# Two of three bit patterns of a key tile summed by an accumulating GpSimd transfer

## The chip, the cores and the metric

The kernel runs on one core of one Trainium2 chip. The metric is the device time of one execution in microseconds. Engines go by their names or by the profile's short ones: TensorE (PE, its weight loads PEld), VectorE (DVE), ScalarE (ACT), GpSimd (POOL) and SyncE (SP, which here only issues transfers).

## The reference

The input x is 2048 rows of 512. It is layer-normalised (no scale, no shift), and the result xn feeds two branches whose product is added to x:

```
q = xn @ wq     32 heads of 16       k, v = xn @ wk, xn @ wv     one head of 16, shared by all 32
s = softmax(q k^T / 4) v, heads joined, @ wo
g = silu( silu(xn @ w1) @ w2 )       w1: 512 x 1792, w2: 1792 x 512
out = x + s * g
```

All inputs and the output are bf16. The large part is the softmax: 32 heads x 2048 queries x 2048 keys, each score exponentiated once.

## The kernel before, in words

The attention is cut into 32 groups: four chunks of 512 queries, and in each eight groups of four heads. A group has 16 key tiles of 128 keys. A **key tile** of a group is four blocks, one a head, each 128 keys x 512 queries. Scores lie transposed (keys on partitions), so a block of exponentials multiplies V directly: a product is one matmul with a 128 x 32 weight (16 columns of V, the rest ones that sum the denominator), and the four heads' products run side by side in four column strips of TensorE. Four such products together are called a quad here. They add up in one PSUM bank per group (`psO`).

A key tile's exponentials are made in one of two ways.

- **ScalarE's tiles.** TensorE writes the scores of two heads into a pair of PSUM banks (`psA`, two pairs in turn, line 613), ScalarE turns 1024 columns at a time into bf16 (`exp_A`, line 643, into one of 11 pieces of `pa_sb`). A tile is two such instructions, and four products, one quad.
- **VectorE's tiles.** TensorE writes one head's scores into one of three banks (`D`, `D1` of `psD`, and `F` = `psF`, which dense work uses too). VectorE adds a constant, clips at zero and writes int16 (`exp_D`, line 681). Read as bf16 these bits are a piecewise linear 2^x. GpSimd adds a constant to the bits of the four blocks at once (`shift`, line 706), once for each of two further patterns, which are the same curve with its kinks elsewhere. The three patterns are weighted and added: each has its own copy of V, scaled by `PH_W`, in `vaug_sb`. So such a tile takes twelve products, three quads. The three patterns of a tile lie in one of `NPD = 4` pattern tiles: three in `ph_sb`, and a fourth in parts of `x_sb` once these are free (`free_slot`, `ph_ap`).

The order of all instructions is written out in Python before the program is built. `Sched.op` appends an instruction to its engine's queue and derives the semaphore waits from what it reads and writes; `Sched.model` keeps an estimated clock for each engine, with fixed costs. A loop at the end goes from one ScalarE exponential to the next: `score_run` sends a burst with ScalarE's next scores and, for heads that are left, scores of VectorE's tiles into free banks (`fill_D`, which starts a new tile through `next_D`); `emit_PV` sends products that the estimated clock says are ready; the rest of TensorE's time goes to the dense jobs (both layers of the gate branch, q projections, the output projection), all in bank `F`. `advance_v` chooses VectorE's next instruction. Parameters of these choices are switched every 5 us of estimated time by a string of letters (`PLAN`, `RULES`). The engines run their queues in order, so what stands in the order is kept on the chip.

Names that matter for the change: `owe` records that a product is still to be made (weight copy `v`, where its block lies, from when it is ready), `owed` and `planned` count the products of a group, `plan_D` adds those of a VectorE tile when it is started. `front` is the list of layer-norm, transposition and k/v work of the start. `left[g]` lists the key tiles of group g that nobody has taken; ScalarE takes from its beginning and VectorE from its end, VectorE only while more than three are left (one in the last group), else from the next group.

Of the kernel before, what the change touches and what calls it, by code (L numbers as in the profile page):

```python
# [6 lines left out]
ALU = mybir.AluOpType  # L7
AX = mybir.AxisListType
FP32 = mybir.dt.float32
BF16 = mybir.dt.bfloat16  # L10
# [5 lines left out]
NQ = 512  # L16
# [3 lines left out]

PH_SHIFT = (0, 43, 85)
PH_W = (0.2265625, 0.1787109375, 0.1416015625)
PH_ONE = 127 * 128
PH_BIAS = 65
NPH = len(PH_SHIFT)
LN2 = 0.6931471805599453
QSCALE = 0.25 * 128.0 / LN2
ESCALE = LN2 / 128.0  # L30
# [5 lines left out]
class Sched:  # L36
# [5 lines left out]
    def __init__(self):  # L42
        self.queues = {}
        self.done = {}
        self.clock = {}
        self.snap = {}
        self.last_w = {}
        self.readers = {}
        self.flagged = {}
        self.lanes = {}  # L50
        self.at = {}
        self.free = dict(pe=1.2, a=1.7, v=0.85, gp=0.7, sp=0.7)
        self.act_end = 0.0
        self.act_ends = []
        self.pe_mode, self.pe_last, self.pe_len, self.pe_tiles = None, 1.0, 0.0, set()
        self.pe_runs = []
        self.gp_runs, self.tt_runs = [], []

    def deps(self, eng, reads, writes):
        deps = {}  # L60
# [33 lines left out]
        return self.pe_last + self.pe_len + (self.SWITCH if mode != self.pe_mode else 0.003)  # L94

    def model(self, eng, lane, cost, r):
        if lane:
            t = max(self.free[eng], r) + 0.05
            self.free[eng] = t
            return t + (cost or 3.0)  # L100
        if eng == "pe":
            mode, tiles, cols = cost or ("full", [None] * 4, 128)
            t = r
            for tile in tiles:
                if mode != self.pe_mode:
                    t = max(t, self.pe_last + self.pe_len + self.SWITCH)
                    self.pe_tiles = set()
                elif tile is not None and tile not in self.pe_tiles:
                    t = max(t, self.pe_last + 0.004)
                else:  # L110
                    t = max(t, self.pe_last + self.pe_len + 0.003)
                    self.pe_tiles = set()
                self.pe_tiles.add(tile)
                self.pe_mode, self.pe_last, self.pe_len = mode, t, max(cols, 60) / 2400.0
                self.pe_runs.append((t, t + self.pe_len))
            self.free[eng] = t
            return t + cols / 2400.0 + self.FLY + self.SEM
        if eng == "a":
            n = cost or 512
            t = max(r, self.free["a"], self.act_end - 0.428)  # L120
            self.free["a"] = t
            self.act_end = max(t + 0.3 + n / 1200.0, self.act_end + 0.0635 + n / 1200.0)
            return self.act_end + self.SEM
        t = max(r, self.free[eng] - (0.084 if eng == "v" else 0.0))
        if eng == "v" and isinstance(cost, tuple):

            t = max(r, self.free[eng] - 0.13)
            end = t + cost[0]
            for a, b in self.gp_runs[-6:]:
                if a < t - 0.1:  # L130
                    end = max(end, b + cost[0] - 0.13)
            self.tt_runs.append((t, end))
            self.free[eng] = end
            return end + self.SEM
        end = t + (cost or 0.4)
        if eng == "gp" and cost and cost > 1.0:
            for a, b in self.tt_runs[-3:]:
                if a <= t + 0.1 and b > t:
                    end = max(end, b + 0.89)
            self.gp_runs.append((t, end))  # L140
        self.free[eng] = end
        return end + self.SEM
# [71 lines left out]
def bass_recurrent_scan__grouped_kv_mqa__dense_activation_silu__prompt_kernel(  # L214
# [22 lines left out]
    assert (S, D, F) == (2048, 512, 1792)  # L237

    NPA = 11
    NPD = 4  # L240
    NPS = 3
    NGN = 2
# [50 lines left out]
    with ExitStack() as es:  # L293
# [46 lines left out]
        K = Sched()  # L340
# [290 lines left out]
        def owe(gi, i, kt, v, ap, key, at, half=None):  # L631
            pend[gi].append(dict(i=i, kt=kt, v=v, ap=ap, key=key, at=at, half=half))
# [40 lines left out]
        def ph_key(j, sl, p):  # L673
            return ("ph", j, sl, p) if sl < 3 else ("x", 4 * j + p)

        def exp_D(blks):

            tile, idx, pos, bank = blks[0]["tile"], blks[0]["idx"], blks[0]["pos"], blks[0]["bank"]
            sl, m = slot_of[idx], 512 * len(blks)
            src = bank_ap(bank, m)  # L680
            d = op("v", lambda e: e.tensor_scalar(ph_ap(0, sl, 512 * pos, 512 * pos + m), src,  # L681
                                                  float(PH_ONE + PH_BIAS), 0.0, op0=ALU.add, op1=ALU.max),
                   reads=[b["bank"] for b in blks], writes=[ph_key(0, sl, b["pos"]) for b in blks],
                   cost=1.221 if len(blks) == 2 else 0.687)
            for b in blks:
                p = b["pos"]
                owe(tile[0], b["i"], tile[1], 1, ph_ap(0, sl, 512 * p, 512 * p + 512).bitcast(BF16), ph_key(0, sl, p), K.at[d])
                hold[b["bank"]] = None
                rows_of.setdefault(idx, {})[p] = b["i"]
            if len(rows_of[idx]) == len(blks[0]["rows"]):  # L690
                if ("ag", NC - 1) in tok:
                    shift(tile, idx)
                else:
                    shifts.append((tile, idx))

        shifts = []

        def shift(tile, idx):
            sl, n = slot_of[idx], len(rows_of[idx])
            for j in range(1, NPH):  # L700
                if n < 4:
                    d = op("v", lambda e, j=j: e.tensor_scalar(ph_ap(j, sl, 0, NQ * n), ph_ap(0, sl, 0, NQ * n), float(PH_SHIFT[j]), None,
                                                               op0=ALU.add),
                           reads=[ph_key(0, sl, p) for p in range(n)], writes=[ph_key(j, sl, p) for p in range(n)], cost=0.4)
                else:
                    d = op("gp", lambda e, j=j: e.int64_add(ph_ap(j, sl, 0, 4 * NQ).bitcast(I64), ph_ap(0, sl, 0, 4 * NQ).bitcast(I64),  # L706
                                                            PH_SHIFT[j] * 0x0001000100010001),
                           reads=[ph_key(0, sl, p) for p in range(4)], writes=[ph_key(j, sl, p) for p in range(4)], cost=1.03)
                for p, i in rows_of[idx].items():
                    owe(tile[0], i, tile[1], 1 + j, ph_ap(j, sl, 512 * p, 512 * p + 512).bitcast(BF16), ph_key(j, sl, p), K.at[d])  # L710

# [67 lines left out]
                state["g"] += 1  # L779
            return n  # L780

        def plan_D(gi, rows):
            owed[gi] += len(rows) * (NPH - 1)
            for i in rows:
                planned[gi][i] += NPH - 1

# [519 lines left out]
        def fill_D(t, free, only=None):  # L1308
# [9 lines left out]
            for bank in banks[:max(0, len(banks) - keep)]:  # L1318
                pick = [(o, i) for o in dst["open"] for i in o["todo"] if i in free]
                if not pick:  # L1320
                    pick = [(o, o["todo"][0]) for o in dst["open"] if o["tile"][0] < group_A() or len(left[o["tile"][0]]) < F_LATE]
                if not pick and len(dst["open"]) < 2:
                    new, rows = next_D(t), [0, 1, 2, 3]
                    if new is not None:
                        left[new[0]].remove(new[1])
                    else:
                        new, rows = next_half(t), [0, 1]
                    if new is not None:
                        plan_D(new[0], rows)
                        dst["idx"] += 1  # L1330
                        slot_of[dst["idx"]] = free_slot(new[0])
                        dst["open"].append(dict(tile=new, todo=list(rows), rows=rows, idx=dst["idx"]))
                        pick = [(dst["open"][-1], i) for i in free if i in rows] or [(dst["open"][-1], rows[0])]
                if not pick:
                    return
                o, i = pick[0]
                pos = len(o["rows"]) - len(o["todo"])
                o["todo"].remove(i)
                if not o["todo"]:
                    dst["open"].remove(o)  # L1340
                burst([((o["tile"], i), bank_ap(bank))], [bank])
                dst["fifo"].append(dict(tile=o["tile"], i=i, bank=bank, idx=o["idx"], pos=pos, rows=o["rows"]))
                hold[bank] = "blk"
                if i not in free:
                    return
                free.remove(i)
                if not free:
                    return
# [171 lines left out]
```

## Time and profile before

| | |
|---|---|
| median of 3 runs | 662.22 us (661.94 to 662.23) |
| the profiled execution | 662.46 us, of it span 660.6 us |
| TensorE clock granted | 1.000 |
| ScalarE exponentials (L643) | 662 of 1024 columns, 630.5 us busy |
| VectorE pattern instructions (L681) | 714, for 724 blocks = 181 key tiles |
| GpSimd shifts (L706) | 362, 374.8 us busy |
| TensorE products (L765) | 2172 of patterns, 1332 of ScalarE's blocks |
| DMA | 12.48 MB, all issued by SP and ACT |

An engine's busy time is the union of its instructions. Matmuls overlap: one takes 383 ns from start to end, but the four of a quad run together and the next quad starts 0.22 us after, so TensorE's 98% counts more than what it could not have done otherwise. In a group's row the figures after the bar are its busy time, the mean of one instruction, and the idle time of the engine just before them with what ended it. In a list of waits the figures are total us, times, and the longest.

### The profile page before, as it was taken

How to read it: one execution, taken by the hardware profiler on the slowest of the kernel's cores; microseconds unless marked ns; L12 is line 12 of the kernel's file. 1: busy time of each engine (PE TensorE's matmuls, PEld its weight loads, DVE VectorE, ACT ScalarE, POOL GpSimd, SP SyncE). 2: the span in 40 equal slices, each digit the busy share in tenths (PEclk: the TensorE clock that was granted, in tenths of full speed). 3: DMA queues.
4: the chain of work that ended last, by engine and by line, in shares of the span. 5: the costliest groups of instructions: out<-in, count | busy, mean ns of one | idle time of the engine just before them, and what ended most of it. 6: DMA issues, size and time to landing. Idle time of an engine off the chain costs nothing.

```text
span 660.6 us, 18424 instructions
## 1 busy us (share of the span) xinstructions
PE 648.8 (98%) x8061; PEld 182.9 (28%) x8061; DVE 597.3 (90%) x1021; ACT 652.5 (99%) x754; POOL 382.9 (58%) x387
## 2 busy tenths in 40 slices
PE   8999999999999999999999999999999999999996
PEld 4422222222222222222222222222222222222222
DVE  7998899998899989999998989999989888898996
ACT  8999999999999999999999999999999999999997
POOL 3265666655566567566656655575656555665554
PEclk9999999999999999999999999999999999999999
DMA  5440000000000000000000000010000000000110
GB/s 167 153 147 1 2 1 2 2 1 2 2 1 2 17 18 18 17 2 2 1 2 1 2 1 2 2 33 18 18 1 3 1 2 2 1 2 2 33 34 33
DMA packets 12320, 12.48 MB, mean 19 GB/s; under 512 B 2512, under 2 KB 11728, under 8 KB 12240
## 3 DMA queue, kind: packets, MB, share of 16 engines
q1 hardware_dynamic: 11680, 10.78, 5.3%
q8 instruction: 63, 1.03, 0.7%
q10 hardware_dynamic: 560, 0.52, 0.2%
q14 instruction: 17, 0.14, 0.1%
HBM read 8.95 MB, written 2.10 MB: 17 GB/s over the span
## 4 chain that ended last, share of the span: by engine, by line
ACT 91%; PE 4%; DVE 2%; issue 1%; DMA 1%; SPq 1%; POOL 0%; POOLq 0%
ACT pa_sb L643 85%; ACT t_sb L1081 5%; PE psA L613 1%; DMA x_sb<-in_A_x_dram 1%; PE psO L765 1%; DVE ph_sb L681 1%; DVE stats_sb L408 0%; POOL ph_sb L706 0%; PE psD L452 0%; PE psF L392 0%; DMA kTb_sb<-kTa_sb 0%; SPq L501 0%; PE psD L483 0%; DVE kTa_sb L495 0%; POOLq L293 0%
## 5 line engine op out<-in xcount | busy, mean ns | idle before, releaser
L643 ACT ACTIVATE pa_sb<-psA 128x1024 bf16<-128x1024 f32 x662 | 630.5, 1217 | 0.9 <-PE psA L613 0.6
L706 POOL INT64_ADD ph_sb<-ph_sb x290 | 300.3, 1048 | 192.7 <-DVE ph_sb L681 192.6
L681 DVE TENSOR_SCALAR ph_sb<-psD 128x512 int16<-128x512 f32 (+1 forms) x520 | 349.1, 689 | 33.7 <-PE psD L613 29.8
L765 PE MATMUL psO<-ph_sb,vaug_sb 128*32 128x512 bf16 x1740 | 215.9, 383 | 0.1
L765 PE MATMUL psO<-pa_sb,vaug_sb 128*32 128x512 bf16 (+1 forms) x1332 | 200.2, 383 | 0.4 <-ACT pa_sb L643 0.4
L613 PE MATMUL psA<-qT_sb,kTa_sb 32*128 32x512 bf16 x688 | 133.4, 385 | 1.9 <-DVE kTa_sb L495 0.5
L613 PE MATMUL psD<-qT_sb,kTb_sb 32*128 32x512 bf16 x353 | 129.5, 384 | 0.0
L613 PE MATMUL psA<-qT_sb,kTb_sb 32*128 32x512 bf16 x628 | 121.7, 385 | 2.2 <-ACT pa_sb L643 1.7
L613 PE MATMUL psD<-qT_sb,kTa_sb 32*128 32x512 bf16 x309 | 111.6, 384 | 0.2
L706 POOL INT64_ADD x_sb<-x_sb x72 | 74.5, 1046 | 52.2 <-DVE x_sb L681 52.1
L681 DVE TENSOR_SCALAR x_sb<-psD 128x512 int16<-128x512 f32 (+1 forms) x132 | 90.1, 690 | 10.6 <-PE psD L613 8.9
L765 PE MATMUL psO<-x_sb,vaug_sb 128*32 128x512 bf16 x432 | 73.7, 383 | 0.0
L613 PEld LDWEIGHTS psA<-qT_sb,kTa_sb 32*128 32x128 bf16 x688 | 32.3, 91 | 141.8 <-ACT pa_sb L643 125.5
L392 PE MATMUL psF<-xnT_sb,w_sb 128*32 128x512 bf16 x896 | 71.1, 385 | 0.0
L392 PE MATMUL psF<-w_sb,u_sb 128*32 128x512 bf16 x896 | 69.2, 384 | 0.0
L613 PEld LDWEIGHTS psA<-qT_sb,kTb_sb 32*128 32x128 bf16 x628 | 29.5, 91 | 134.4 <-ACT pa_sb L643 124.4
L765 PEld LDWEIGHTS psO<-ph_sb,vaug_sb 128*32 128x32 bf16 x1740 | 52.5, 95 | 49.7 <-issue 34.1
L765 PEld LDWEIGHTS psO<-pa_sb,vaug_sb 128*32 128x32 bf16 x1332 | 48.1, 94 | 41.9 <-issue 32.1
L1081 ACT ACTIVATE t_sb<-psF 128x512 bf16<-128x512 f32 x72 | 57.4, 797 | 0.0
L1113 DVE SCALAR_TENSOR_TENSOR u_sb<-t_sb,psF 128x512 bf16<-128x512 bf16 x56 | 38.0, 679 | 4.7 <-ACT t_sb L1081 4.2
L681 DVE TENSOR_SCALAR ph_sb<-psF 128x512 int16<-128x512 f32 x52 | 35.4, 681 | 0.0
L613 PEld LDWEIGHTS psD<-qT_sb,kTb_sb 32*128 32x128 bf16 x353 | 30.9, 91 | 3.5 <-DVE ph_sb L681 2.5
(128 smaller groups left out, 341.6 us busy)
## 6 DMA issues: line engine op xcount, KB each, us to landing
w_sb<-in_B_w_dram SPq DMA_DIRECT2D x2, 1792.0 KB, 8.8
x_sb<-in_A_x_dram SPq DMA_DIRECT2D x18, 128.0 KB, 2.3
out_dram<-ob_sb SPq DMA_DIRECT2D x14, 128.0 KB, 1.7
x_sb<-in_A_x_dram SPq DMA_DIRECT2D x3, 512.0 KB, 7.1
wop_sb<-in_A_wo_dram SPq DMA_DIRECT2D x1, 512.0 KB, 4.0
wq_sb<-in_A_wq_dram SPq DMA_DIRECT2D x1, 384.0 KB, 6.6
x_sb<-in_A_x_dram ACTq DMA_DIRECT2D x2, 128.0 KB, 2.9
kTb_sb<-kTa_sb SPq DMA_DIRECT2D x16, 16.0 KB, 2.3
```

What stands on the lines that cost most here:

```text
L392: r = e.matmul(bank[32 * i:32 * i + 32, :], lhsT=lhsT[:, 32 * i:32 * i + 32], rhs=rhs, start=start, stop=stop, tile_position=(0, 32 * i), ...
L613: return e.matmul(ap, lhsT=kT_sb[g % 2][32 * i:32 * i + 32, kt * P:(kt + 1) * P], rhs=qT_sb[32 * i:32 * i + 32, c % 2, g // 2, :], start=T ...
L643: d = op("a", lambda e: e.activation(pa_sb[:, sl, :], psA[k][:, :], ACT.Exp, scale=ESCALE), reads=["A%d" % k], writes=[("pa", sl)], cost=2 ...
L681: d = op("v", lambda e: e.tensor_scalar(ph_ap(0, sl, 512 * pos, 512 * pos + m), src, float(PH_ONE + PH_BIAS), 0.0, op0=ALU.add, op1=ALU.ma ...
L706: d = op("gp", lambda e, j=j: e.int64_add(ph_ap(j, sl, 0, 4 * NQ).bitcast(I64), ph_ap(0, sl, 0, 4 * NQ).bitcast(I64), PH_SHIFT[j] * 0x0001 ...
L765: r = e.matmul(psO[32 * i:32 * i + 32, cs], lhsT=vaug_sb[:, p["v"], p["kt"], :], rhs=p["ap"], start=s0, stop=s1, tile_position=(0, 32 * i) ...
L1081: op("a", lambda e: e.activation(t_sb[:, n % 2, :], bank_ap(b), ACT.Tanh, scale=0.5 if jb[0] == "h" else 0.25), reads=[b], writes=[("t", n ...
L1113: op("v", lambda e: e.scalar_tensor_tensor(out=dst, in0=t_sb[:, n % 2, :], scalar=1.0, in1=src, op0=ALU.add, op1=ALU.mult), reads=tk["read ...
```

## The change

Patterns 0 and 1 get the same weight (0.1953125), with shifts 0, 42 and 88 in place of 0, 43 and 85; the constant of line 681 moves from 65 to 67. With equal weights the two patterns can be added first and multiplied once. For the tiles in the set `summed`, GpSimd issues a transfer right after it has made pattern 1: source pattern 0, destination pattern 1, with `accum_op` add in bf16, 128 partitions of 4 KB. Then it makes pattern 2 as before. Products of pattern 0 are left out, products of "pattern 1" read the sum and wait for the transfer. Such a tile takes eight products, two quads.

A tile is in `summed` if it has all four heads, the front is over, and it is either of a later group than the one ScalarE is in or leaves at least `SUML = 6` tiles of its group untaken. The model counts the issue as 1.0 us of GpSimd, then 2.6 us in a row of such transfers, then 2.0 us to landing. The string of letters and all other parameters stay.

```diff
-PH_SHIFT = (0, 43, 85)
-PH_W = (0.2265625, 0.1787109375, 0.1416015625)
+PH_SHIFT = (0, 42, 88)
+PH_W = (0.1953125, 0.1953125, 0.1416015625)
 PH_ONE = 127 * 128
-PH_BIAS = 65
+PH_BIAS = 67
+SUM_ISSUE, SUM_TIME, SUM_LAND = 1.0, 2.6, 2.0
...
     def model(self, eng, lane, cost, r):
+        if lane and eng == "gp":
+            t = max(self.free[eng], r) + SUM_ISSUE
+            self.free[eng] = t
+            self.sums = max(self.sums + cost, t + cost)
+            return self.sums + SUM_LAND
...
+    SUML = 6
...
             for b in blks:
                 p = b["pos"]
-                owe(tile[0], b["i"], tile[1], 1, ph_ap(0, sl, 512 * p, 512 * p + 512).bitcast(BF16), ph_key(0, sl, p), K.at[d])
+                if idx not in summed:
+                    owe(tile[0], b["i"], tile[1], 1, ph_ap(0, sl, 512 * p, 512 * p + 512).bitcast(BF16), ph_key(0, sl, p), K.at[d])
...
+                if idx in summed and j == 1:
+                    d = op("gp", lambda e: e.dma_start(ph_ap(1, sl, 0, 4 * NQ).bitcast(BF16), ph_ap(0, sl, 0, 4 * NQ).bitcast(BF16),
+                                                       accum_op=ALU.add),
+                           reads=[ph_key(0, sl, p) for p in range(4)], writes=[ph_key(1, sl, p) for p in range(4)],
+                           lane=f"sum{sl}", cost=SUM_TIME)
...
-        def plan_D(gi, rows):
-            owed[gi] += len(rows) * (NPH - 1)
+        def plan_D(gi, rows, n):
+
+            owed[gi] += len(rows) * (n - 1)
             for i in rows:
-                planned[gi][i] += NPH - 1
+                planned[gi][i] += n - 1
...
                     if new is not None:
-                        plan_D(new[0], rows)
                         dst["idx"] += 1
+                        if not front and len(rows) == 4 and (new[0] > group_A() or len(left[new[0]]) >= SUML):
+                            summed.add(dst["idx"])
+                        plan_D(new[0], rows, NPH - (dst["idx"] in summed))
```

More of the change, by code (lines that the diff above doesn't have):

```diff
@@ L57, in __init__ @@
         self.gp_runs, self.tt_runs = [], []
+        self.sums = 0.0
     def deps(self, eng, reads, writes):
@@ L694, in exp_D @@
                     shifts.append((tile, idx))
-        shifts = []
+        shifts, summed = [], set()
         def shift(tile, idx):
```

## The prediction

> **What bounds the kernel now.** I read the page's shares of the engines and the chain that ended last, then its groups, the busy times by stretch, the list of waits, and last the DMA rows. Shares, chain, groups and DMA rows, from the page (a group's columns: line, engine, operation, count, busy us, mean ns, idle us before it and what ended that):
>
> ```profile
> PE 648.8 (98%) x8061; PEld 182.9 (28%) x8061; DVE 597.3 (90%) x1021; ACT 652.5 (99%) x754; POOL 382.9 (58%) x387
> ...
> ACT 91%; PE 4%; DVE 2%; issue 1%; DMA 1%; SPq 1%; POOL 0%; POOLq 0%
> ...
> L643 ACT ACTIVATE pa_sb<-psA 128x1024 bf16<-128x1024 f32 x662 | 630.5, 1217 | 0.9 <-PE psA L613 0.6
> L706 POOL INT64_ADD ph_sb<-ph_sb x290 | 300.3, 1048 | 192.7 <-DVE ph_sb L681 192.6
> L681 DVE TENSOR_SCALAR ph_sb<-psD 128x512 int16<-128x512 f32 (+1 forms) x520 | 349.1, 689 | 33.7 <-PE psD L613 29.8
> L765 PE MATMUL psO<-ph_sb,vaug_sb 128*32 128x512 bf16 x1740 | 215.9, 383 | 0.1
> ...
> x_sb<-in_A_x_dram SPq DMA_DIRECT2D x3, 512.0 KB, 7.1
> wop_sb<-in_A_wo_dram SPq DMA_DIRECT2D x1, 512.0 KB, 4.0
> ```
>
> ScalarE is never short of work: 91% of the chain, and 0.9 us of idle before all its 662 exponentials. A key tile there is two of them (331 tiles); the other 181 of 512 are VectorE's. So the end moves in two ways only: VectorE takes more or fewer tiles, or something makes ScalarE wait. In the chain's longest pieces 28 exponentials take 25.67 us, 0.917 us each: one tile moved to or from ScalarE is 1.84 us.
>
> Busy time by stretch (us, then each engine's busy us and count, the granted clock, DMA):
>
> ```profile
> 100.00:200.00 100.00, 99.14 (x1243) 27.12 (x1244) 89.28 (x144) 100.00 (x118) 57.91 (x57) 1.00 0.01 2
> 200.00:300.00 100.00, 99.71 (x1260) 26.91 (x1256) 93.29 (x158) 100.00 (x115) 63.07 (x61) 1.00 0.04 12
> ```
>
> The third busy figure is VectorE's: 89 to 94% in every middle stretch, with ScalarE at 100. Over 20 to 640 us it sums to 567.7 of 620 (91.6%). What it waits for, and who waits for GpSimd's shifted patterns:
>
> ```profile
> DVE ph_sb L681 <- PE psD L613: 29.8, 113, 1.0
> DVE x_sb L681 <- PE psD L613: 8.9, 31, 0.6
> ...
> PEld psO L765 <- POOL ph_sb L706: 4.6, 20, 0.4
> ```
>
> VectorE loses 38.7 us to score banks that are not filled yet. Of 362 shifted patterns only 24 (20 here and 4 of the tile in x_sb) were waited for by a product: products lie in TensorE's queue, so a pattern may come somewhat late today.
>
> **Baseline.** The profiled execution took 662.46 us: span 660.6, and 1.9 around it. The median is 662.22, 0.24 lower; I sum changes and add them to 662.2.
>
> **Which tiles.** 181 VectorE tiles over 32 groups are 5.7 a group. The rule leaves out tiles taken when fewer than six of the group's 16 remain after it; taking stops at three. Of the 13 removals in which they are taken about 3 fall there: 10/13 x 181 = 139, a few lost before 50 us and a few won by tiles of the next group, which always count. I take 140 of 181 (77%).
>
> **Products: 140 fewer quads.** A line of the timeline shows 12 such products (three quads) in 0.83 us, one quad in 0.39: 0.22 us a quad. 140 x 0.22 = 31 us less TensorE work, all off the chain. What it can buy is limited by VectorE's waits for banks. A VectorE tile costs four pattern instructions, 2.66 us (349.1 + 35.4 + 90.1 + 6.8 us for 181); to give ScalarE back 1.84 us, VectorE needs 2.66 + 1.84 = 4.5 us of its idle time, so 1 us of it is worth 0.41. All waits: 38.7 x 0.41 = 16 us. But a fill is sent together with ScalarE's own scores, which wait until the exponential two before has released its bank. From the records of the trace I took, for each wait of over 0.05 us before a pattern instruction (44 us), how late that burst began after the release plus the shortest delay seen, some 0.06 to 0.09 us: 12.7 us in all. Only that can be TensorE's fullness: 12.7 x 0.41 = 5.2 us. Bounds: -16 to 0; faster at best 5, if VectorE still has a tile to write into.
>
> **GpSimd: 140 issues.** The transfer is issued between the two shifts, so the third pattern's shift stands behind it, and the issue itself behind the first shift. Before has no DMA on that queue, so no row prices it: nearest are its shortest fill, 0.31 us, and two shifts in a row, 2.1. I take 1.0, as one shift (1.05). Load 383 + 140 = 523 us of 660; hidden below 1.8 us an issue ((640 - 383)/140), and SP's queue is not passed. Other waits on GpSimd's queue: none but the shifts of the next tile, which today leave it idle 245 us.
>
> **The transfer.** 140 x 512 KB. The load queue moved 10.78 MB in 5.3% of 16 engines' span, 35 us, so 512 KB is 1.7 us of all engines as a copy, 3.4 if the destination is read too, against one summed tile every 4.7 us: no jam. Landing: bounds 4.0 us (the quiet 512 KB row) to 7.1 (the crowded one). Nearest is the quiet row, plus part of the second read: 5.0. By the Trainium skill, page "DMA: Bandwidth & Descriptors", section "Anatomy of one DMA — SWDGE (gpsimd) path", such a transfer takes about 2.0 us plus its bytes at 436 GB/s: 3.2 us for 512 KB, an estimate, and no run here shows a transfer of that queue. The sum by it would be the first rival's 657, since tiles would then come free in time; the quiet row of 4.0 is already longer than that page's figure, so I keep the row.
>
> **The tile that is held.** This decides. VectorE has four pattern tiles (three, and one in x_sb). Following each through the records, in the order the kernel lists them: from the first pattern instruction to the last product 10.3 us on average, 4.0 of it filling; between 100 and 600 us a tile is begun every 3.45 us (145 in 500), so 3.0 are in use, all four 20% of the time. After its last block a tile has the first shift at 1.13 us and the second at about 2.25, and then its products queue a median of 2.8 us. Now the sum is there at 1.13 + 1.0 + 5.0 = 7.1 us, 4.9 later than the last pattern today. The queue may shorten; TensorE's freed time is one tenth of its column work (31 of about 313 us), and dense work takes what is free, so I allow a quarter, 0.75 us. Hold of a summed tile 10.3 + 4.9 - 0.75 = 14.4 us, mean with the others 0.77 x 14.4 + 0.23 x 10.3 = 13.5. At 3.45 us a tile that is 3.9 of 4 in use on average, which a fluctuating order doesn't reach; I take 3.8 (nearer to 4 than to the 3.0 of now, because VectorE has other work while a tile is late). Then one every 13.5/3.8 = 3.55 us: over 600 us 169 in place of 174, 4.9 fewer. ScalarE gets them at 1.84 us, and the longer run lets VectorE win some back: 4.9 x 1.84/(1 + 1.84/3.55) = 5.9 us. With landing 4.0 and the queue halved (-1.5) the hold is 12.2 us, 3.5 in use: nothing. With 3.6 usable: +17. With landing 7.1 and the queue as it is, 15.7 us: one every 4.1, 28 tiles fewer, +36. The gain on banks then has no tile to be spent on.
>
> **Sum:** 662.2 + 5.9 = 668.1, about 668.
>
> **Rivals.**
> (1) Faster: tiles come free in time (mean hold under 13.1 us, 3.8 x 3.45), and fuller bursts earlier give 5.2 us: 657; were all bank waits to go, 646. For it: no wait for a tile shows today, and TensorE is full by every stretch. Against: ScalarE's pace, not TensorE, sets two thirds of those waits.
> (2) A late landing: the order is written before the run, and TensorE takes it in turn. It counts 1.0 + 2.6 + 2.0 us from the issue. If the chip needs more than this and the queue's 2.8 us, a product stands at the head of TensorE's queue, scores behind it are late and ScalarE idles. From a landing of about 7.4 us after the issue on, each 0.1 us costs up to 140 x 0.1 = 14 us; with half the cushion gone the point is 6.0, and the crowded row's 7.1 would give over 700. Against: no crowd after 60 us (DMA share 0.01 to 0.04).
> (3) GpSimd becomes the bound: an issue that waits for two of VectorE's 0.68 us instructions takes 1.0 + 1.4 = 2.4 us, and 383 + 140 x 2.4 = 719 us pass the span; VectorE then gets fewer tiles, some 690. Against: one such wait, 1.7 us, still fits, and the int64 adds show no wait of this kind beside the same instructions (1037 ns median, 1315 at most). By the Trainium skill, page "SBUF — State Buffer", section "SBUF: two separate sides", GpSimd cannot write a transfer's descriptors while VectorE runs in its two-port mode. No run here shows it for a transfer.
> (4) Nothing: tiles cost as much as banks win, 661 to 663.5.
>
> **Chances.** About 0.2% is what a measurement can tell. Held tiles 0.40 (664 to 682), late landing 0.11, GpSimd 0.03: slower 0.54. Faster 0.38, mostly 651 to 660. Same 0.08. The range that leaves out 2 in 10 is 651 to 692: a twelfth below, the dear end of (2) and of the hold above. The slower case's own range is 664 to 692.
>
> **What would show it.** Products of patterns near 1600 in place of 2172; 140 transfers; ScalarE's exponentials: 672 or so (slower), under 655 (faster). VectorE's pattern instructions with idle before them ended by a product or a transfer, not by a filled bank, prove the held tile. Rows of TensorE waiting for the transfer, with idle before ScalarE's exponentials in place of 0.9 us, prove (2). Wrong I would be if the landing is near 4 us, or if the queue in front of the products drains.

## The result, and the profile after

The changed kernel takes 714.23 us, median of 3 runs (714.02 to 719.28), against 662.22: a ratio of 1.081 (1.077 to 1.086), 52.0 us slower. The profiled execution took 714.23 us, of it span 712.0, at a granted clock of 0.997. Within one kernel, runs at a clearly lower granted clock took longer (here 719.28 us at 0.988 and 714.02 at 0.997), so differences of a few us are read between runs at like clocks.

From the page after, the shares of the engines, the chain, the groups and the DMA rows (columns as before):

```profile
PE 670.8 (94%) x8020; PEld 190.8 (27%) x8027; DVE 583.8 (82%) x935; ACT 684.1 (96%) x784; POOL 475.6 (67%) x492
...
ACT 38%; PE 24%; DVE 19%; POOL 12%; issue 3%; DMA 3%; SPq 0%; POOLq 0%
...
L651 ACT ACTIVATE pa_sb<-psA 128x1024 bf16<-128x1024 f32 x692 | 655.5, 1127 | 18.6 <-PE psD L621 10.5
L715 POOL INT64_ADD ph_sb<-ph_sb x258 | 303.7, 1249 | 140.4 <-DVE ph_sb L689 140.4
L689 DVE TENSOR_SCALAR ph_sb<-psD 128x512 int16<-128x512 f32 (+1 forms) x434 | 302.2, 715 | 52.0 <-PE psD L621 48.5
...
L719 POOL DMA_DIRECT2D ph_sb<-ph_sb x103 | 90.4, 878 | 33.4 <-POOL ph_sb L715 30.7
...
L400 PE MATMUL psO<-zero_sb 128*32 128x512 bf16 x636 | 47.5, 386 | 0.0
...
ph_sb<-ph_sb POOLq DMA_DIRECT2D x103, 512.0 KB, 4.6
x_sb<-x_sb POOLq DMA_DIRECT2D x32, 512.0 KB, 4.6
```

Three things are to be seen. ScalarE has 692 exponentials where it had 662: VectorE lost 15 tiles (166 left). ScalarE, 91% of the chain before, is 38% of it now, and 18.6 us of idle lie before its exponentials where 0.9 lay. And TensorE's freed work bought nothing: 636 matmuls on a tile of zeros (24 before) stand in the order where it found TensorE nothing else to do.

The span's growth of 51.4 us is ScalarE's busy time, +31.6 (652.5 to 684.1; 30 exponentials at 0.917 are 27.5 of it), and ScalarE's idle time, +19.8 (660.6 - 652.5 = 8.1 before, 712.0 - 684.1 = 27.9 after). These two parts have different causes, and the experiments part them: the number of exponentials is fixed when the order is written, the idle time arises on the chip. The 4.1 us of busy time that the count leaves over are met again below.

The stretches after, in the columns of before:

```profile
100.00:200.00 100.00, 96.21 (x1173) 26.63 (x1166) 78.21 (x124) 97.75 (x115) 63.79 (x64) 1.00 0.52 99
200.00:300.00 100.00, 95.97 (x1165) 26.77 (x1157) 86.53 (x137) 98.25 (x113) 74.22 (x76) 1.00 0.67 132
```

VectorE falls from 89 and 93 us to 78 and 87 of each 100, ScalarE from 100 to 98; nothing became fuller but GpSimd and the DMA engines. The waits after:

```profile
DVE ph_sb L689 <- PE psD L621: 48.5, 102, 3.6
...
POOL ph_sb L719 <- POOL ph_sb L715: 30.7, 101, 1.0
DVE tmp_sb L1128 <- ACT t_sb L1096: 26.6, 11, 4.4
...
PEld psD L621 <- DVE ph_sb L689: 16.7, 35, 2.0
...
PEld psO L779 <- POOL ph_sb L715: 11.7, 29, 1.0
ACT pa_sb L651 <- PE psD L621: 10.5, 15, 1.9
...
PEld psO L779 <- DMA ph_sb<-ph_sb: 3.0, 7, 1.1
```

Products waiting for the transfer itself are a small row, 3.0 us in `ph_sb`. What grew is TensorE waiting for VectorE to release a score bank: 16.7 us in 35 waits of up to 2.0, where the trace of before has this row:

```profile
PEld psD L613 <- DVE ph_sb L681: 6.7, 27, 0.4
```

Behind such a wait in TensorE's queue stand ScalarE's next scores, hence the exponentials' 10.5 us on psD. VectorE must be late for that, by up to 2 us at once. The timeline of VectorE and that of GpSimd after show such a place (start, duration, engine, line; in brackets the idle time before it):

```profile
408.18 0.23 DVE L859 RECIPROCAL rcp_sb<-otr_sb 128x16 f32<-128x16 f32 x1
408.33 0.63 DVE L689 TENSOR_SCALAR ph_sb<-psD 128x512 int16<-128x512 f32 x1
408.88 1.86 DVE L868 TENSOR_TENSOR onb_sb<-otr_sb,rcp_sb 128x256 bf16<-128x256 f32 x1
410.66 0.68 DVE L689 TENSOR_SCALAR ph_sb<-psD 128x512 int16<-128x512 f32 x1
```

```profile
407.15 1.04 POOL L715 INT64_ADD ph_sb<-ph_sb  x1 [1.02 <-DVE ph_sb L689]
408.49 0.87 POOL L719 DMA_DIRECT2D ph_sb<-ph_sb  x1 [0.30 <-POOL ph_sb L715]
409.09 1.36 POOL L715 INT64_ADD ph_sb<-ph_sb  x1
```

The division of line 868 reads two operands from SBUF and takes 0.41 us when nothing is in its way. Here it starts 0.39 us after an issue and ends 0.29 us after the end of the shift behind that issue (410.74 against 410.45): 1.86 us. The one-operand instructions of line 689 beside it keep their 0.6 to 0.7.

### The profile page after: what moved, and what is told of

Read it like the earlier page. It is cut to its first block, busy times and chain, and to the rows that moved or that the text cites. A ratio compares the mean times of both kernels' runs of the same rounds, so it can differ in the third digit from the quotient of the medians.

```text
span 712.0 us, 18438 instructions
## 1 busy us (share of the span) xinstructions
PE 670.8 (94%) x8020; PEld 190.8 (27%) x8027; DVE 583.8 (82%) x935; ACT 684.1 (96%) x784; POOL 475.6 (67%) x492
## 3 DMA queue, kind: packets, MB, share of 16 engines
q0 software_dynamic: 19440, 70.79, 52.4%
## 4 chain that ended last, share of the span: by engine, by line
ACT 38%; PE 24%; DVE 19%; POOL 12%; issue 3%; DMA 3%; SPq 0%; POOLq 0%
ACT pa_sb L651 35%; DVE ph_sb L689 9%; PE psA L621 8%; POOL ph_sb L715 6%; PE psF L400 6%; PE psO L779 6%; ACT t_sb L1096 3%; DVE onb_sb L868 3%; POOL x_sb L715 3%; POOL ph_sb L719 2%; PE psO L400 2%; DVE x_sb L689 2%; DMA ph_sb<-ph_sb 1%; DVE otr_sb L851 1%; DVE ob_sb L1107 1%
## 5 line engine op out<-in xcount | busy, mean ns | idle before, releaser
L651 ACT ACTIVATE pa_sb<-psA 128x1024 bf16<-128x1024 f32 x692 | 655.5, 1127 | 18.6 <-PE psD L621 10.5
L689 DVE TENSOR_SCALAR ph_sb<-psD 128x512 int16<-128x512 f32 (+1 forms) x434 | 302.2, 715 | 52.0 <-PE psD L621 48.5
L779 PE MATMUL psO<-pa_sb,vaug_sb 128*32 128x512 bf16 (+1 forms) x1392 | 174.2, 384 | 3.0 <-POOL ph_sb L715 1.3
L779 PE MATMUL psO<-ph_sb,vaug_sb 128*32 128x512 bf16 x1136 | 143.3, 384 | 2.8 <-POOL ph_sb L715 1.9
L719 POOL DMA_DIRECT2D ph_sb<-ph_sb x103 | 90.4, 878 | 33.4 <-POOL ph_sb L715 30.7
L621 PE MATMUL psD<-qT_sb,kTb_sb 32*128 32x512 bf16 x314 | 100.3, 384 | 7.0 <-DVE ph_sb L689 5.9
L715 POOL INT64_ADD x_sb<-x_sb x74 | 92.0, 1250 | 20.4 <-DVE x_sb L689 20.3
L689 DVE TENSOR_SCALAR x_sb<-psD 128x512 int16<-128x512 f32 (+1 forms) x129 | 90.4, 713 | 15.3 <-PE psD L621 13.4
L621 PE MATMUL psD<-qT_sb,kTa_sb 32*128 32x512 bf16 x285 | 93.7, 386 | 1.8 <-DVE ph_sb L689 1.7
L779 PE MATMUL psO<-x_sb,vaug_sb 128*32 128x512 bf16 x316 | 47.0, 385 | 1.4 <-POOL x_sb L715 0.7
L400 PE MATMUL psO<-zero_sb 128*32 128x512 bf16 x636 | 47.5, 386 | 0.0
```

The costliest lines, as they stand in the source:

```text
L400: r = e.matmul(bank[32 * i:32 * i + 32, :], lhsT=lhsT[:, 32 * i:32 * i + 32], rhs=rhs, start=start, stop=stop, tile_position=(0, 32 * i), ...
L621: return e.matmul(ap, lhsT=kT_sb[g % 2][32 * i:32 * i + 32, kt * P:(kt + 1) * P], rhs=qT_sb[32 * i:32 * i + 32, c % 2, g // 2, :], start=T ...
L651: d = op("a", lambda e: e.activation(pa_sb[:, sl, :], psA[k][:, :], ACT.Exp, scale=ESCALE), reads=["A%d" % k], writes=[("pa", sl)], cost=2 ...
L719: d = op("gp", lambda e: e.dma_start(ph_ap(1, sl, 0, 4 * NQ).bitcast(BF16), ph_ap(0, sl, 0, 4 * NQ).bitcast(BF16), accum_op=ALU.add), read ...
L779: r = e.matmul(psO[32 * i:32 * i + 32, cs], lhsT=vaug_sb[:, p["v"], p["kt"], :], rhs=p["ap"], start=s0, stop=s1, tile_position=(0, 32 * i) ...
```

## The experiments

The theory on record, the held tile, had to be told from three others: that the order lost something else than tiles (the string of letters was chosen for another order), that the transfer is late or crowds the DMA engines, and that the issue on GpSimd's queue delays others. Ratios are to the kernel before, run on the same chip, with 95% intervals.

**The constants alone.** No tile is put in `summed`.

```diff
-                        if not front and len(rows) == 4 and (new[0] > group_A() or len(left[new[0]]) >= SUML):
+                        if False:
```

> The changed kernel with no tile summed: only the shifts, weights and the constant of VectorE's instruction differ from before. All theories: the order is that of before, 662.2 us, within 0.3%. If the time moves, the constants or the equal weights carry part of the 52 us.

662.09 us, 1.000 (0.999 to 1.001), 662 exponentials. The constants cost nothing; all 52 us belong to the summed tiles.

**The string of letters.** Both kernels with one letter throughout.

```diff
-    PLAN = (
...
+    PLAN = "A" * 150
```

> The kernel before with the letter A for every stretch, so with nothing fitted. Theory 'fitted order' (the string of letters fits only the one order that it was made with, and any other order loses it): 675 to 685 us, with some 9 VectorE tiles fewer than 181, ScalarE's exponentials near 680, and ScalarE idle little more than 8 us. Theory 'held tile alone' (the sum's tiles are held for 15 us and VectorE goes short of them): the letters matter little, 662 to 667 us.

> The changed kernel with the letter A for every stretch. 'Held tile alone': as the changed kernel, 710 to 718 us, about 50 over the plain kernel before. 'Fitted order' together with the held tile: about 700 to 708, only 25 to 30 over the plain kernel before, of which some 10 for tiles (fewer exponentials would say less) and some 20 for a third pattern that comes later than the order says (ScalarE idle near 28 us in place of 8).

The kernel before becomes 678.85 us (1.025, 1.024 to 1.027): 680 exponentials, 172 tiles, with no transfer in it. The changed kernel stays where it was, 712.52 (1.076, 1.074 to 1.077). So the letters are worth 16.7 us to the order they were chosen with, and nothing to the new one, which is 1.7 us faster without them. Between the two plain kernels lie 33.7 us, more than the 25 to 30 expected: ten exponentials (9.2 us, 5 tiles), ScalarE's idle time, 8.0 against 28.7, and some 5 us more that ScalarE is busy.

**How easily the fit is lost.** `may_D` refuses to write a block while products of an earlier tile in the same pattern tile are pending. In the order after, a start is refused 145 times (44 different blocks), in that of before 4 times (3 blocks; counted while the order is written). Here the second and third pattern are looked at only for a tile's last block, so that a tile may start earlier:

```diff
-            return not any(held(ph_key(j, sl, p)) for j in range(1, NPH) for p in range(4)) and \
+            full = len(rows_of.get(blks[0]["idx"], {})) + len(blks) == len(blks[0]["rows"])
+            return not (full and any(held(ph_key(j, sl, p)) for j in range(1, NPH) for p in range(4))) and \
```

> The kernel before, in which VectorE may begin to refill a pattern tile while products of its second and third pattern are still to come, and only the last block waits for them; in the order of before this lifts just four refusals. 'Fitted order': the slight shift of the order loses the fit, 675 to 685 us. 'Held tile alone': 660 to 662 us, since no tile was short.

> The changed kernel in which VectorE may begin to refill a pattern tile while products of its second and third pattern are still to come; only the last block of the tile waits for them. Theory 'held tile': of the 30 exponentials more than before it takes back about 12 (6 key tiles), and the time falls from 714 to 699 to 705 us, the lateness staying as it is. Theory 'order's fit alone': another order of the same worth, 708 to 720 us, exponentials 686 or more.

In the kernel before, lifting four refusals costs 19.3 us: 681.53 (1.029, 1.027 to 1.031), 681 exponentials. A permission that only adds choices made it worse, by about as much as dropping the letters did. In the changed kernel it wins 19.6 us: 694.65 (1.051, 1.046 to 1.056), 680 exponentials in place of 692. That is better than the 699 to 705 expected. Twelve exponentials, 11 us, come back as the held tile would have it; the other 8 us are less idle time, which wasn't expected. One pair of orders can't tell how much of the twelve is the tile and how much another order's luck, since the same edit moved the kernel before by 19.

**One pattern tile fewer, before.** `NPD = 4` becomes 3.

> The kernel before with three pattern tiles in place of four; no transfer. Its letters lose their fit, as in the kernel before with the late check, 681.5 us. 'Held tile' (tiles short of what VectorE wants cost its share): clearly over that, 696 to 702 us, with some 700 exponentials and VectorE's tiles near 161. If tiles are not the limit: 678 to 684 us.

698.80 us (1.055, 1.054 to 1.057), 701 exponentials: 17.3 us and 20 exponentials more than the unfitted order with four tiles (681.53). Tiles in use do set VectorE's share. A fifth tile, the opposite test, wasn't tried.

**The order without the transfer, and with a small one.** First the order of the changed kernel, instruction by instruction, with an add of 8 numbers in place of the transfer. Then the same order with the transfer cut to 8 numbers a partition, 0.29 MB in all.

```diff
-                    d = op("gp", lambda e: e.dma_start(ph_ap(1, sl, 0, 4 * NQ).bitcast(BF16), ph_ap(0, sl, 0, 4 * NQ).bitcast(BF16),
-                                                       accum_op=ALU.add),
...
+                    d = op("gp", lambda e: e.int64_add(scr_i[:, :].bitcast(I64), scr_i[:, :].bitcast(I64), 1),
```

> The changed kernel in the same order, instruction for instruction, but where it issues the transfer GpSimd adds 1 to eight numbers of a scratch tile: the sum is left out (products of pattern 1 read pattern 1 alone), and nothing waits for a landing. What remains of the 52 us belongs to the order: theory 'order and execution' (the order itself costs some 30 us by tiles that ScalarE took over, 692 exponentials in place of 662, and the rest is time that the chip is late against the order): 690 to 695 us, ScalarE idle near 8 us. Theory 'order alone': 710 to 715 us, ScalarE idle near 28 as now.

> The changed kernel in the same order, with the transfer cut to the first eight numbers of each partition (the sum of the rest is left out): the issue on GpSimd stays, the bytes go. Theory 'issue' (GpSimd's time for the issue, the third pattern behind it and VectorE's two-operand instructions that wait for it make the chip late): 708 to 715 us, as the changed kernel, issue rows near 0.87 us, two-operand rows of 1 us. Theory 'landing' (sums that land late stop TensorE): as the kernel without the transfer, 690 to 697 us.

The page without the transfer:

```profile
PE 664.9 (96%) x8027; PEld 189.0 (27%) x8027; DVE 564.2 (82%) x935; ACT 680.3 (99%) x784; POOL 375.6 (54%) x492
...
L652 ACT ACTIVATE pa_sb<-psA 128x1024 bf16<-128x1024 f32 x692 | 655.9, 1183 | 1.3 <-PE psA L622 0.6
```

691.95 us (1.045, 1.043 to 1.047): the same 692 exponentials and 1.3 us of idle before them. The order costs 29.7 us, its execution with the transfer 22.3 more. ScalarE is busy 680.3 us here, so of its 31.6 us of added busy time 27.8 are the order's and 3.8 come with the transfer. The tiles that would be summed are held about 14.5 us here too, for about 15 with the transfer, though nothing lands: their products stand that late in TensorE's queue. The page with the small transfer:

```profile
PE 673.4 (95%) x8027; PEld 190.8 (27%) x8027; DVE 584.1 (82%) x935; ACT 684.3 (96%) x784; POOL 476.2 (67%) x492
...
L651 ACT ACTIVATE pa_sb<-psA 128x1024 bf16<-128x1024 f32 x692 | 655.5, 1128 | 19.1 <-PE psD L621 10.2
...
ph_sb<-ph_sb POOLq DMA_DIRECT2D x103, 2.0 KB, 2.0
```

716.79 us (1.083, 1.078 to 1.088), nothing won, though the transfers land after 2.0 us and no longer load the DMA engines. So neither landing nor bytes make the 22.3 us. What is left is the issue, with what stands behind it.

**What in the issue.** It does two things: the third pattern comes later (the second shift is done 3.40 us after the tile's last block, 2.15 before), and GpSimd runs something that others may wait for. The first was tested alone, by short fills in the issue's place, first 9, then 21 of them:

```diff
+                    d = op("gp", lambda e: [e.memset(pad_sb[:, 11 * m:11 * m + 11], 0.0) for m in range(21)][-1],
```

> The changed kernel in the same order, with nine short fills of a scratch tile on GpSimd in place of the transfer, together about as long (the sum is left out). They hold up the second shift as an issue does, but read nothing and are no transfer. Theory 'late third pattern': the chip stays late, 708 to 718 us, as with the issue. Theory 'two-operand instructions' (only a transfer's issue holds VectorE's additions and products for 1.9 us): 692 to 698 us, near the kernel with no transfer, and those rows at 0.4 to 1.0 us.

> As the kernel with nine fills in place of the transfer, in the changed kernel's order, but with 21 of them, since nine turned out at half an issue's time (second shift done 2.76 us after the tile's last block, 3.40 with an issue). Theory 'late third pattern': with the second shift done at 3.4 us the chip is late as with the issue, 708 to 718 us. Theory 'two-operand instructions': 693 to 699, as with nine fills.

693.84 us (1.048, 1.047 to 1.050) and 693.21 (1.046, 1.044 to 1.049): 1.9 and 1.3 us above the order without transfer. With nine fills the second shift was done at 2.76 us, too early for the question; with 21 at 3.16, all but 0.24 us of the issue's delay. A late third pattern costs next to nothing up to there, and the two-operand rows stay at 1.27 us and less. The counterpart is a small transfer issued behind both shifts, so that the patterns are as early as before (2.15 us):

```diff
+                if idx in summed and j == 2:
+                    q = K.queues["gp"]
+                    q[-2], q[-1] = q[-1], q[-2]
```

> The changed kernel's order, but on GpSimd's queue each issue stands behind the tile's second shift in place of ahead of it, and the transfer is cut to eight numbers a partition (the rest of the sum is left out), so that it lands in time. Theory 'late third pattern': the lateness goes, 692 to 698 us. Theory 'two-operand instructions': they still meet issues, 703 to 716 us, with rows over 1 us as many as with the issue ahead, if shorter ones.

707.69 us (1.068, 1.066 to 1.070). With the third pattern on time, 15.7 us of 22.3 are still there, though some of it can be the granted clock: 0.988 to 0.991 in these runs, 0.998 to 1.000 in those without the transfer. Rows over 1 us are nine, not as many as with the issue ahead (15), and the longest is 3.04 us.

**Who waits for the issue.** VectorE's instructions with two operands in SBUF are the 31 divisions and the additions to `ob_sb`. Their groups by form, before:

```profile
L853 DVE TENSOR_TENSOR onb_sb<-otr_sb,rcp_sb 128x256 bf16<-128x256 f32 x31 | 15.1, 489 | 0.0
...
L1092 DVE TENSOR_TENSOR ob_sb<-fin_sb,x_sb 128x512 bf16<-128x512 bf16 x12 | 5.3, 442 | 0.0
```

and after:

```profile
L868 DVE TENSOR_TENSOR onb_sb<-otr_sb,rcp_sb 128x256 bf16<-128x256 f32 x31 | 31.7, 1023 | 0.1
...
L1107 DVE TENSOR_TENSOR ob_sb<-fin_sb,x_sb 128x512 bf16<-128x512 bf16 x12 | 12.6, 1059 | 0.1
```

By what GpSimd does when one of the 47 starts (these groups, two more additions and two short divisions): nothing, 0.41 us (median of 20); a shift, 0.80 (17); an issue, 1.92 (8, from 1.72 to 2.03); an issue and the shift behind it at once, 1.50 and 2.48 (2). All ten issues have a shift right behind them. With the small transfer issued behind both shifts that isn't always so, and the timelines of that run part the two. In the first two rows (VectorE's, then GpSimd's) nothing stands behind the issue, in the last three the next tile's shifts do:

```profile
431.04 0.42 DVE L871 TENSOR_TENSOR onb_sb<-otr_sb,rcp_sb 128x256 bf16<-128x256 f32 x1
430.95 0.86 POOL L719 DMA_DIRECT2D ph_sb<-ph_sb  x1
...
597.00 3.01 DVE L871 TENSOR_TENSOR onb_sb<-otr_sb,rcp_sb 128x256 bf16<-128x256 f32 x1
596.75 0.87 POOL L719 DMA_DIRECT2D ph_sb<-ph_sb  x1 [0.61 <-POOL ph_sb L715]
597.36 2.36 POOL L715 INT64_ADD x_sb<-x_sb  x2
```

Five rows of that run start during an issue with no shift right behind it and take 0.41 to 0.42 us. Four start during an issue with two shifts behind it and take 2.61 to 3.01, ending 0.29 us after the second shift. So the issue alone holds nothing up; the shift that stands behind it does, and from before its own row begins. How it does so that early isn't shown.

The test of what these waits cost keeps order and transfers and gives the 43 rows of the two groups one operand:

```diff
-            op("v", lambda e: e.tensor_tensor(d3, o3, rcp_sb[:, sl, :].unsqueeze(2).to_broadcast([P, NQ // 32, DH]), ALU.mult),
+            op("v", lambda e: e.bn_stats(bnx_sb[:, 2 * so + b, :], otr_sb[:, sl, 0:256]),
...
+                op(eng, lambda e: e.bn_stats(bnx_sb[:, 4 + slot, :], src[:, 0:256]),
```

> The changed kernel with its transfers, in the same order; only VectorE's 31 products of two SBUF tiles (the division of the attention output) and 12 additions (x to the result) are replaced by row statistics over 256 numbers, which read one tile and take about as long when nothing disturbs them (0.41 us). The division and those additions are left out. Theory 'two-operand instructions': the lateness goes with them, 692 to 698 us, ScalarE idle 9 to 13 us in place of 28. Theory 'third pattern or something else in the issue': 708 to 716.

Its groups, and then its waits:

```profile
L869 DVE BATCH_NORM_STATS2 bnx_sb<-otr_sb 128x6 f32<-128x256 f32 x31 | 12.9, 415 | 0.1
...
L1109 DVE BATCH_NORM_STATS2 bnx_sb<-fin_sb 128x6 f32<-128x256 bf16 x12 | 4.9, 413 | 0.1
```

```profile
PEld psO L780 <- POOL ph_sb L716: 13.5, 33, 1.1
...
PEld psO L780 <- DMA ph_sb<-ph_sb: 5.0, 8, 1.3
PE psO L780 <- POOL ph_sb L716: 4.5, 12, 0.8
PEld psD L622 <- DVE ph_sb L690: 4.3, 18, 0.3
```

698.69 us (1.055, 1.053 to 1.057), just over the 692 to 698 expected, with ScalarE idle 15.9 us for the 9 to 13 expected. The rows keep 0.41 us beside the same issues, and TensorE's wait for a bank falls from 16.7 us, longest 2.0, to 4.3, longest 0.3. So 15.5 of the 22.3 us are VectorE's two-operand instructions waiting for GpSimd (14.4 to 14.6 between runs at the same granted clock, 0.997). The other 6.7 aren't settled: products still wait for shifts and transfers, but neither the late shift (to 3.16 us) nor the bytes showed a price of their own when each was tried alone.

**Telling the order.** Three runs change what the order believes. With one letter throughout, the issue is counted 1.2 us and the landing 1.8 (the sum unchanged); then also GpSimd's issue and the shift after it are told to the rule that the order already has for VectorE's two-operand instructions:

```diff
-SUM_ISSUE, SUM_TIME, SUM_LAND = 1.0, 2.6, 2.0
+SUM_ISSUE, SUM_TIME, SUM_LAND = 1.2, 2.6, 1.8
...
+            self.gp_runs.append((t - SUM_ISSUE, t + 1.03))
```

> The changed kernel with the letter A throughout, its order told that an issue takes 1.2 us of GpSimd in place of 1.0 and that the landing comes 0.2 earlier after it. Against the plain changed kernel, 712.5 us. Theory 'late third pattern' (it comes 0.2 us later than the order says and stops TensorE): most of the lateness goes, 684 to 692 us, ScalarE idle near 10. Theory 'two-operand instructions' (VectorE's additions and products of two tiles in SBUF wait for the issue and the shift behind it, 1.9 us in place of 0.4, which the order does not know): still 703 to 713.

> As the plain one with the issue at 1.2 us, and the order also told that VectorE's two-operand instructions wait for an issue and the shift behind it, as it is already told of shifts. 'Two-operand instructions': the lateness goes, ScalarE idle near 10 us and the time near 692 to 698, more exponentials than in the plain changed kernel and yet shorter. 'Late third pattern': no better than the plain one with the issue at 1.2 us.

698.15 us (1.054, 1.050 to 1.059) and 700.77 (1.058, 1.057 to 1.060), where the plain changed kernel took 712.52. The first has 685 exponentials for 690 and 16.1 us of idle time for 28.7; why 0.2 us of belief does so much isn't shown, the whole order is another. Its runs went from 694.17 us at a granted clock of 1.000 to 701.00 at 0.989, but at like clocks the gap stays: 711.33 us at 0.988 for the plain one. The second halves the idle time (13.6) although its two-operand rows stay long (47.4 us), since the order now allows for them; but it pays with 694 exponentials. The first time lies in neither theory's range, and the second is above the 692 to 698 expected and no better than the first, so these two orders decide nothing between the theories.

Last, both kernels with letters chosen anew from all "A" by the order's own estimate, the changed one with the late check and the issue at 1.2:

> The kernel before, its letters thrown away and fitted anew from the letter A, by the order's own estimate of its end (some thousand tries). All theories: between the plain 678.9 and 662.2 us; I expect 673 to 677, some 674 exponentials. It is the measure for the changed kernel fitted alike.

> The changed kernel with the late check and the issue counted as 1.2 us, its letters fitted anew from the letter A with the same effort. Theory 'fit plus two-operand instructions': the order is worth about as much as the one of before fitted alike (exponentials within 6 of it), but the chip is late against it: 681 to 689 us, ScalarE idle 18 to 24 us. If the change paid once fitted: at or below the kernel before fitted alike.

676.61 us (1.024, 1.020 to 1.028) and 692.26 (1.048, 1.043 to 1.052). Fitted alike, the two orders are level: 676 exponentials before, 674 after, ScalarE busy 665.8 and 666.4 us. On the chip the changed one is 15.6 us slower, and past the 681 to 689 expected, with 23.3 us of ScalarE's idle time against 9.5. The original string's 662 was not reached again, and no version beat the kernel before.

**The runs by the two causes.** Exponentials come from the order. The idle time (span less ScalarE's busy time) goes on the whole with the time of the 47 two-operand rows; the exception is the last kernel, whose order allows for them. The run with one operand isn't listed, since 43 of its rows are others.

| kernel | exponentials | the 47 rows, us | ScalarE idle, us |
|---|---|---|---|
| before | 662 | 21.9 | 8.1 |
| after, no tile summed | 662 | 21.9 | 7.9 |
| before, one letter | 680 | 24.5 | 8.0 |
| before, refitted | 676 | 24.6 | 9.5 |
| order of after, 21 fills | 692 | 25.1 | 12.0 |
| before, late check | 681 | 25.6 | 9.4 |
| order of after, no transfer | 692 | 26.4 | 9.2 |
| before, three pattern tiles | 701 | 27.3 | 8.6 |
| order of after, nine fills | 692 | 28.9 | 10.8 |
| after, issue 1.2, one letter | 685 | 35.4 | 16.1 |
| after, small transfer behind the shifts | 692 | 38.4 | 24.1 |
| after, late check | 680 | 40.7 | 20.0 |
| after, refitted | 674 | 41.0 | 23.3 |
| after | 692 | 45.9 | 27.9 |
| after, small transfer | 692 | 46.2 | 28.1 |
| after, one letter | 690 | 47.9 | 28.7 |
| after, order told, one letter | 694 | 47.4 | 13.6 |

## Why the prediction was wrong

It had the direction and one of the mechanisms, and named 668 us, range to 692, where 714 came. By its steps:

- **Which tiles** held: 135 summed of 166 (81%), for 140 of 181.
- **Products.** Fewer, as counted: 1452 of patterns in place of 2172 (4 x 135 by the sums, 12 x 15 by the tiles lost). The step's remark that the gain has no tile to be spent on came true: the waits for filled banks rose from 38.7 us to 61.9 (48.5 and 13.4).
- **The transfer** held: landing 4.6 us in the median and 4.9 on average, for 5.0; no jam, at 52.4% of the DMA engines for 70.79 MB. The 4.6 include the issue, which the step of the held tile adds once more: the sum was there 6.5 us after a tile's last block, not 7.1. The Trainium skill's estimate by its page "DMA: Bandwidth & Descriptors", section "Anatomy of one DMA — SWDGE (gpsimd) path", was 3.2; its fixed part of about 2.0 us agrees with the 2.0 of the 2 KB transfers, so it is the accumulating 512 KB that take longer than its rate.
- **The tile that is held**: hold of a summed tile 15.0 us (14.4), of the others 10.3 (10.3). The step put the hold down to the chip's landing. But without any transfer the same order holds these tiles about 14.5 us: it counts 5.6 us (1.0 + 2.6 + 2.0) from the issue to the landing and places the products by that. The second shift of before, read as 2.25 us after the last block, was at 2.15. The like-for-like pair with one letter lost 5 tiles, for 4.9, which is in part luck, since the share in use was mis-sized: 3.53 of 4 tiles between 100 and 600 us and not 3.8, with one begun every 4.10 us and not 3.55; and a tile that is lost isn't won back: ten exponentials, 9.2 us, for 5.9. The sign given for it also failed: VectorE's idle time still ends by filled banks, because the order doesn't start a tile that isn't free, and no wait remains to be seen on the chip.
- **The baseline under that step** failed. It took one tile every 3.45 us as what the machine gives, when it was what one string of letters gives for one exact order. Without that fit the kernel before has 680 or 681 exponentials, 16.7 or 19.3 us, and nothing of this size stood in the sum. The order's 29.7 us are then about 17 to 19 of lost fit and 10 to 13 of held tiles; the split rests on those neighbours, since the two can't be taken apart within one order.
- **GpSimd: 140 issues** had the price about right (0.87 us and 0.30 of waiting for the shift before it, for 1.0; the shortest fill of before took 0.10 us, not 0.31) and the load somewhat high (475.6 us busy, for 523). The step that failed is that it missed who waits for GpSimd. "Other waits on GpSimd's queue: none" looked at what GpSimd waits for. The trace of before already held the sign: 10 of its 47 two-operand rows took over 0.6 us, with a median of 0.61 beside a shift and 0.41 beside none. These waits are 15.5 us of the result.
- **Rival (2)**, the late landing, is refuted by the small transfer. **Rival (3)** had the contention the wrong way round: not GpSimd waited for VectorE, VectorE waited for GpSimd. By the Trainium skill, page "SBUF — State Buffer", section "Who interferes with whom", a VectorE instruction with two SBUF inputs contends with a GpSimd instruction that reads SBUF. The 0.80 us beside a shift agree with it. The same section says that one which only writes doesn't contend. The fills agree: 14 such instructions that started beside them alone took 0.38 to 0.42 us. The issue alone held none up either, 0.41 to 0.42 us for five; the 1.92 us are the wait for the shift behind it.

## What to carry to other kernels

When a kernel's order was fitted choice by choice, price its unfitted neighbour first: a neutral perturbation of the kernel before cost 2.5 to 2.9%. When work is added to GpSimd's queue, list not only what it waits for but every VectorE instruction with two SBUF operands, and look up in the trace what those rows take beside GpSimd's work and alone, and what stands in GpSimd's queue behind the new work. To part an order's cost from its execution, run the same order with the new operation swapped for one that does almost nothing.

## What the runs showed of the hardware

- A two-operand VectorE instruction that starts during GpSimd's issue of a transfer waits when a shift stands right behind the issue: 1.50 to 2.48 us in place of 0.41 (ten rows), the end 0.3 us after a shift's. With two shifts behind the issue it was 2.61 to 3.01 us (four rows), with none 0.41 to 0.42 (five).
- The shift behind an issue has a row of 1.36 us in place of 1.04, which begins 0.27 us before the issue's row ends.
- 512 KB added in bf16 from SBUF to SBUF land 4.6 us after the start of the issue (4.5 to 7.8), 2 KB in 2.0. Each of the large ones took 52.4% x 712.0 / 135 = 2.8 us of all 16 DMA engines, against 1.7 by the load queue's share for a copy of that size.
